# Attention, routed experts and a feed-forward layer on one core: v's two heads of a pair in one product, two v buffers instead of three

## The chip, the cores and the metric

One core of a Trainium2 chip runs the whole program. The metric is device microseconds (us) of one execution, the median of several runs. Five engines work side by side, each through its own list of instructions in order: TensorE (PE, matrix products; its weight loads are shown as PEld), VectorE (DVE), ScalarE (ACT), GpSimd (POOL) and SyncE (SP, which here only starts transfers). They wait for each other through semaphores.

## The reference

```python
# attention: q, k, v of (4 batches, 8 heads, 576 tokens, 64)
q_d, k_d, v_d = mean over groups of 4 tokens        # 144 "downsampled" tokens
out_d  = softmax(scale * q_d @ k_d.T) @ v_d
out_up = repeat(out_d, 4, axis=tokens)
mask   = abs(pos_i - pos_j) < 4
out_local = softmax(where(mask, scale * q @ k.T, -1e9)) @ v
x = (out_up + out_local), heads side by side: (2304, 512)
# routing: each token goes to the expert with the largest cosine logit
y = gate * (relu(x @ w1[e]) @ w2[e])                # 8 experts, 512 -> 1024 -> 512
# feed-forward
h = y @ w_in; out = maximum(0.01 * h, h) @ w_out    # 512 -> 2048 -> 512
```

## The kernel before, in words

The program has two stretches. In the first, the attention and the routing are worked through in 18 tiles of 128 tokens (the four batches laid end to end, 4.5 tiles each). In the second the tokens go expert by expert through the expert layers and then through the feed-forward layer, as long runs of 384- and 512-wide matmuls.

The order of the first stretch is written out by hand in the table ORDER: a list of steps like `LV.6` or `vw.3`, each a call of one function. Each engine runs its share of the steps in the order of the table; transfers of SP too, since they are issued where the step stands. A scheduler does not change it. The steps that matter here:

- `T`, `E`, `P`: q and k are transposed on PE, copied out of PSUM, and added up by fours into qd and kd.
- `ds` is dn_score (L390, L395): downsampled scores of one batch, in two parts; then `dm`, `db`, `dx` (softmax), `dT`, `dv` (dn_pv, L439 and L445: times v_d), `do`, `dh`, `dl` (the result, split into a high part dnh and a low part dnl).
- `S` is lo_score: the local scores. A tile is four strips of 32 queries; each strip meets a window of 38 keys. `SMX` to `SNM` are its softmax, `LT` and `LTE` transpose it into leT, in which the two heads of a pair lie on partitions 0 to 63 and 64 to 127.
- `vw` is load_vw (L319, L323): the windows of v for nine strips (a group, 0 to 7, two per batch) go into one of NVW buffers `vw`, in turn, as 10 or 12 transfers on SP. Head s of a pair lies on partitions 64 s to 64 s + 63. The buffers are set to zero once (L196), since a window fills 48 of 64 partitions. Tile t reads groups 4t // 9 to (4t + 3) // 9: tile 4 reads groups 1 and 2, tile 6 groups 2 and 3, tile 13 groups 5 and 6, tile 15 groups 6 and 7.
- `LV` is lo_pv: the local result of a tile and the repeated downsampled result, added up in one PSUM tile psLV. First the repeat products, with a constant matrix rep_w that copies each downsampled row four times (L554; rows 512 to 575 of a batch, in the four tiles that cross a batch, go through rem_w instead, L559), once for each of the two head halves; then for each of 4 head pairs, 2 heads and 4 strips one small product of leT and vw (L567). A float32 matmul here appears as two records, each a weight load and a pass.
- `LX`, `LAD`: the tile is copied to xt and stored to memory. `SQ`, `X`, `XE`, `L`, `LG`, `LD`, `PF`, `PD`, `SC`: the routing (logits, arg-max, ranks, scattering of the token numbers), for three tiles at a time from `LD` on.
- `WL.u` is w_moe_load for the first expert: SP loads unit u of its weights (two transfers of 512 KB). `WH.u` and `WO.u` split them into a high part (a cast on ACT, L866) and a low part (a subtraction on DVE, L869), in four pieces. The raw weights lie in two buffers, the split ones in four (pools wa and wb, two each).
- `XT`, `XH`, `XO` bring the first tokens of the first expert into place; `L1.f` is its first layer for 128 columns f. `L1.2` and `L1.3` need unit 1.

Of the kernel before, what the change touches and what calls it, by code (L numbers as in the profile page):

```python
# [8 lines left out]
F32 = mybir.dt.float32  # L9
# [44 lines left out]
O = dict(QM=(0, 0, 1, 1), NQ=8, NQD=2, NDE=0, NC=0, NVD=2, NVW=3, NES=3, NW=22, TO=12, TS=11, HB=2, XF=4, XL=3.0, WL=4,  # L54
# [18 lines left out]
E.2.1.1.1 L.3 db.1.1 S.7 SNM.6 LTE.4 LG.3 P.2.1.1 dv.1.0 dx.1.1 ds.2.0 v.2.0 SMX.7 dT.1.1.0 do.1.0 T.2.0.1.1 dE.1.1.0
SSB.7 dT.1.1.1 E.2.0.1.1 dT.1.1.2 dh.1.0 SEX.7 S.8 dm.2.0 dE.1.1.2 dl.1.0 X.1 dE.1.1.1 P.2.0.1 db.2.0 T.3.1.0.0 XE.1
dv.1.1 SMX.8 dx.2.0 E.3.1.0.0 SSB.8 v.2.1 T.3.1.1.0 SSM.7 SEX.8 dT.2.0.0 LAD.1 T.3.1.0.2 do.1.1 LAD.0 dE.2.0.0 ds.2.1
vg.3.0 E.3.1.0.2 E.3.1.1.0 qk.3.0.1 dh.1.1 SSM.8 dT.2.0.1 LAD.2 T.3.1.1.1 dE.2.0.1 dl.1.1 T.3.0.0.0 LAD.3 SNM.8 L.1
vg.3.1 E.3.1.1.1 dm.2.1 T.3.0.0.1 SNM.7 E.3.0.0.0 LV.5 LG.1 E.3.0.0.1 db.2.1 dv.2.0 LX.5 LD.2 v.3.0 dx.2.1 LV.4 LAD.5
# [32 lines left out]
def tile_kernel(ctx, tc, q, k, v, emb, tau, w1, w2, win, wout, out):  # L110
# [51 lines left out]
    with man:  # L162
# [28 lines left out]
        vws = [ac.tile([P, NP, GS, D], F32, name="vw%d" % i) for i in range(O['NVW'])]  # L191
# [119 lines left out]
        def load_vw(g):  # L311
# [3 lines left out]
            for s in range(2):  # L315
                part = t[64 * s:64 * s + 64]
# [67 lines left out]
        def dn_score(b, u):  # L384
            ps = psA.tile([P, 2, 512], F32, name="psD", tag="A")
            idle(ps[:, 0, 0:256], dn_score, b, u)
            for r in range(2):
                for c in range(0, P, 64):
                    for s in range(2):
                        T.matmul(ps[c:c + 64, s, r * GR:(r + 1) * GR], qd[b][64 * s:64 * s + 64, 2 * u + r, c:c + 64],  # L390
                                 kd[b][64 * s:64 * s + 64, 2 * u + r, :], start=True, stop=True)
            if u:
                for n in range(NP):
                    for s in range(2):
                        T.matmul(ps[32 * n:32 * n + 32, s, 2 * GR:3 * GR],  # L395
                                 qd[b][64 * s:64 * s + 64, n, GR - 32:], kd[b][64 * s:64 * s + 64, n, :],
                                 start=True, stop=True)
            sps[b, u] = ps
# [31 lines left out]
        def dn_pv(b, u):  # L430
# [109 lines left out]
        def lo_pv(t):  # L540
# [773 lines left out]
```

## Time and profile before

| | |
|---|---|
| median of 3 runs | 858.31 us (855.56 to 859.88) |
| profiled execution, its own time | 853.95 us |
| its span, first to last instruction | 852.2 us |
| PE busy | 810.4 us (95%), 7887 matmul records |
| DVE, ACT, POOL busy | 462.5, 337.2, 210.7 us |
| mean granted clock of PE | 0.971 |
| DMA | 97.88 MB; 58956 of 104652 packets under 512 B |

The granted clock is 1.0 where PE runs at 2.4 GHz and 0.5 where it runs at 1.2. "Idle before" is the time an engine stood still ahead of an instruction, with what ended it; "issue" means that nothing which the profile shows was awaited.

### The profile page before, as it was taken

How to read it: one execution, taken by the hardware profiler on the slowest of the kernel's cores; microseconds unless marked ns; L12 is line 12 of the kernel's file. 1: busy time of each engine (PE TensorE's matmuls, PEld its weight loads, DVE VectorE, ACT ScalarE, POOL GpSimd, SP SyncE). 2: the span in 40 equal slices, each digit the busy share in tenths (PEclk: the TensorE clock that was granted, in tenths of full speed). 3: DMA queues.
4: the chain of work that ended last, by engine and by line, in shares of the span. 5: the costliest groups of instructions: out<-in, count | busy, mean ns of one | idle time of the engine just before them, and what ended most of it. 6: DMA issues, size and time to landing. Idle time of an engine off the chain costs nothing. (4 is left out here: it accounts for less than half of the span.)

```text
span 852.2 us, 19006 instructions
## 1 busy us (share of the span) xinstructions
PE 810.4 (95%) x7887; PEld 742.1 (87%) x7887; DVE 462.5 (54%) x902; ACT 337.2 (40%) x686; POOL 210.7 (25%) x244
## 2 busy tenths in 40 slices
PE   7878999789999999999999999999999999999995
PEld 6767787679999999999997789999999999999994
DVE  6646655544377988897579992332332232232222
ACT  3445645544454555656433232322223222222221
POOL 8465534234033234323023420101001001001001
PEclk9989978979999999999999999999999999999998
DMA  9779654545476787797634410111011011000001
GB/s 266 172 173 193 157 124 98 140 131 123 102 267 191 258 237 212 237 293 238 211 113 125 136 50 1 37 38 38 1 38 38 0 38 38 1 1 38 0 1 40
DMA packets 104652, 97.88 MB, mean 115 GB/s; under 512 B 58956, under 2 KB 83148, under 8 KB 104562
## 3 DMA queue, kind: packets, MB, share of 16 engines
q1 hardware_dynamic: 94018, 69.88, 29.8%
q0 software_dynamic: 10544, 26.74, 9.9%
q8 instruction: 64, 1.05, 0.5%
q14 instruction: 26, 0.21, 0.1%
HBM read 81.48 MB, written 15.12 MB: 113 GB/s over the span
## 5 line engine op out<-in xcount | busy, mean ns | idle before, releaser
L923 PE MATMUL psh<-xhi,w 128*128 128x384 f32 (+9 forms) x672 | 215.9, 321 | 0.0
L924 PE MATMUL psh<-xlo,w 128*128 128x384 f32 (+9 forms) x672 | 215.6, 321 | 0.0
L925 PE MATMUL psh<-xhi,w 128*128 128x384 f32 (+9 forms) x672 | 215.2, 320 | 0.0
L955 DVE SCALAR_TENSOR_TENSOR hs<-hs 128x384 f32<-128x384 f32 x96 | 61.9, 645 | 185.8 <-ACT hs L954 185.8
L923 PEld LDWEIGHTS psh<-xhi,w 128*128 128x128 f32 x672 | 127.7, 190 | 4.0
L924 PEld LDWEIGHTS psh<-xlo,w 128*128 128x128 f32 x672 | 127.7, 190 | 3.9
L925 PEld LDWEIGHTS psh<-xhi,w 128*128 128x128 f32 x672 | 127.6, 190 | 0.0
L954 ACT COPY hs<-psh 128x384 f32<-128x384 f32 x96 | 45.9, 478 | 194.5 <-PE psh L925 191.6
L1008 PE MATMUL pso<-w,hh 128*128 128x512 f32 x282 | 112.9, 400 | 3.7 <-ACT hh L960 3.1
L1009 PE MATMUL pso<-w,hh 128*128 128x512 f32 x282 | 110.9, 393 | 0.0
L1039 POOL DMA_INDIRECT out_dram<-o,tk x18 | 18.0, 999 | 320.9 <-ACT o L1038 315.4
L869 DVE TENSOR_TENSOR w<-r,w 128x1024 fp32r<-128x1024 f32 (+1 forms) x72 | 83.1, 1159 | 11.0 <-ACT w L866 10.6
L960 ACT CAST hh<-hs 128x384 fp32r<-128x384 f32 x94 | 48.2, 513 | 93.2 <-DVE hs L955 93.2
L996 PE MATMUL psy<-hh,w 128*128 128x192 f32 (+8 forms) x288 | 81.9, 306 | 0.0
L1006 PE MATMUL pso<-w,hl 128*128 128x512 f32 x282 | 80.8, 393 | 0.0
L997 PE MATMUL psy<-hh,w 128*128 128x192 f32 (+8 forms) x288 | 79.4, 298 | 0.0
L911 POOL TENSOR_TENSOR ds<-r 128x512 f32<-128x512 f32 x32 | 42.5, 1327 | 145.8 <-DVE r L909 63.5
L961 DVE TENSOR_TENSOR hl<-hs,hh 128x384 fp32r<-128x384 f32 x94 | 52.4, 557 | 45.8 <-ACT hh L960 45.8
L975 ACT ACTIVATE hh<-psh 128x192 fp32r<-128x192 f32 (+8 forms) x72 | 29.2, 405 | 110.4 <-PE psh L925 107.3
L866 ACT CAST w<-r 128x1024 fp32r<-128x1024 f32 (+1 forms) x72 | 67.6, 947 | 3.5 <-DMA r<-in_moe_w_dram 3.5
L1008 PEld LDWEIGHTS pso<-w,hh 128*128 128x128 f32 x282 | 52.9, 188 | 16.9 <-ACT hh L960 7.9
L1006 PEld LDWEIGHTS pso<-w,hl 128*128 128x128 f32 x282 | 53.0, 188 | 12.9 <-DVE hl L961 0.3
(230 smaller groups left out, 1255.2 us busy)
## 6 DMA issues: line engine op xcount, KB each, us to landing
r<-in_moe_w_dram SPq DMA_DIRECT2D x64, 512.0 KB
r<-in_moe_w_in_dram POOLq DMA_DIRECT2D x16, 512.0 KB, 5.3
r<-in_moe_w_out_dram POOLq DMA_DIRECT2D x16, 512.0 KB, 5.0
vw<-in_v_dram SPq DMA_DIRECT2D x64, 96.0 KB
vg<-in_v_dram SPq DMA_DIRECT2D x8, 576.0 KB
x_d<-xt SPq DMA_DIRECT2D x18, 256.0 KB
yc<-yT_d SPq DMA_DIRECT2D x6, 768.0 KB
qk<-in_q_dram SPq DMA_DIRECT2D x4, 576.0 KB
```

The lines of the kernel that those rows point to most:

```text
L866: A.copy(w[:, 0, i, cs], src)
L869: V.tensor_tensor(out=w[:, 1, i, cs], in0=src, in1=w[:, 0, i, cs].bitcast(F32), op=ALU.subtract)
L923: T.matmul(ps, lh, rh, start=start, stop=False)
L924: T.matmul(ps, lh, rl, start=False, stop=False)
L925: T.matmul(ps, ll, rh, start=False, stop=stop)
L955: V.scalar_tensor_tensor(out=hs, in0=hs, scalar=0.01, in1=hs, op0=ALU.mult, op1=ALU.max)
L961: V.tensor_tensor(out=gl[:, 0:n], in0=hs, in1=gh[:, 0:n].bitcast(F32), op=ALU.subtract)
L996: T.matmul(ps, wh, hh[:, 0:n], start=f == 0, stop=False, skip_group_check=True)
L997: T.matmul(ps, wl, hh[:, 0:n], start=False, stop=False, skip_group_check=True)
L1006: T.matmul(ps, hl[:, c], wh, start=False, stop=f == NF2 - 1, skip_group_check=True)
L1008: T.matmul(ps, hh[:, c], wh, start=f == 0, stop=False, skip_group_check=True)
L1009: T.matmul(ps, hh[:, c], wl, start=False, stop=False, skip_group_check=True)
```

## The change

Four things change together. The buffers of v get a column block for each head of a pair: head 0 fills partitions 0 to 63 of block 0, head 1 partitions 64 to 127 of block 1, and the rest stays zero. One product over all 128 partitions and 128 columns then gives both heads of a pair, where there were two of 64 by 64; the repeat products become 512 (or 128) wide, once instead of once per half, and psLV takes one bank of PSUM instead of two. A buffer is now twice as large, so there are two instead of three (NVW), and the loads of v stand at other places in ORDER. The room for this comes from the split weights of the first stretch: pool wa has one buffer until `cut`, a new pool wc gets the other after it, and the splits of unit 1 (`WH.1`, `WO.1`) stand behind `XH.3`. In dn_score, the products of 64 columns become products of 128.

```diff
-O = dict(..., NVD=2, NVW=3, ...
+O = dict(..., NVD=2, NVW=2, ...
...
-        vws = [ac.tile([P, NP, GS, D], F32, name="vw%d" % i) for i in range(O['NVW'])]
+        vws = [ac.tile([P, NP, GS, 2, D], F32, name="vw%d" % i) for i in range(O['NVW'])]
...
-                part = t[64 * s:64 * s + 64]
+                part = t[64 * s:64 * s + 64, :, :, s]
...
             for r in range(2):
-                for c in range(0, P, 64):
-                    for s in range(2):
-                        T.matmul(ps[c:c + 64, s, r * GR:(r + 1) * GR], qd[b][64 * s:64 * s + 64, 2 * u + r, c:c + 64],
-                                 kd[b][64 * s:64 * s + 64, 2 * u + r, :], start=True, stop=True)
+                for s in range(2):
+                    T.matmul(ps[:, s, r * GR:(r + 1) * GR], qd[b][64 * s:64 * s + 64, 2 * u + r, 0:P],
+                             kd[b][64 * s:64 * s + 64, 2 * u + r, :], start=True, stop=True)
...
-            for s in range(2):
-                for z, (b, r, p0) in enumerate(segs):
-                    for w, src in enumerate((dn_h[b], dn_l[b])):
-                        if r < 4 * P:
-                            T.matmul(ps[:, s, 0:256], rep_w[:, HW + r - p0:HW + r - p0 + P],
-                                     src[:, 0:DM].rearrange("p (i a d) -> p a i d", i=2, a=2)[:, s],
-                                     start=z == 0 and w == 0, stop=False, skip_group_check=True)
-                        else:
-                            for n in range(NP):
-                                T.matmul(ps[:, s, n * D:(n + 1) * D], rem_w[:, n, HW - p0:HW - p0 + P],
-                                         src[:, DM + s * D:DM + (s + 1) * D],
-                                         start=z == 0 and w == 0 and n == 0, stop=False, skip_group_check=True)
+            for z, (b, r, p0) in enumerate(segs):
+                for w, src in enumerate((dn_h[b], dn_l[b])):
+                    first = z == 0 and w == 0
+                    if r < 4 * P:
+                        T.matmul(ps[:, 0], rep_w[:, HW + r - p0:HW + r - p0 + P], src[:, 0:DM],
+                                 start=first, stop=False, skip_group_check=True)
+                    else:
+                        for n in range(NP):
+                            T.matmul(ps[:, 0, 2 * n * D:2 * (n + 1) * D], rem_w[:, n, HW - p0:HW - p0 + P],
+                                     src[:, DM:DM + 2 * D], start=first and n == 0, stop=False, skip_group_check=True)
 
             for n in range(NP):
-                for s in range(2):
-                    for c, b, sg, w0 in strips(t):
-                        w = vwt[b * (NSTRIP // GS) + sg // GS][:, :, sg % GS]
-                        T.matmul(ps[32 * c:32 * c + 32, s, n * D:(n + 1) * D],
-                                 eT[64 * s:64 * s + 64, n, 32 * c:32 * c + 32], w[64 * s:64 * s + 64, n, :],
-                                 start=False, stop=True, skip_group_check=True)
+                for c, b, sg, w0 in strips(t):
+                    w = vwt[b * (NSTRIP // GS) + sg // GS]
+                    T.matmul(ps[32 * c:32 * c + 32, 0, 2 * n * D:2 * (n + 1) * D], eT[:, n, 32 * c:32 * c + 32],
+                             w[:, n, sg % GS].rearrange("p s d -> p (s d)"), start=False, stop=True, skip_group_check=True)
...
-            for nm, bufs in (("wa", 2), ("xa", 1), ("rp", 1)):
+            for nm, bufs in (("wa", 1), ("xa", 1), ("rp", 1)):
...
-            for nm, bufs in (("wb", 2), ("wf", 4), ("rr", 2), ("xb", 1), ("hp", 2)):
+            for nm, bufs in (("wb", 2), ("wf", 4), ("rr", 2), ("xb", 1), ("hp", 2), ("wc", 1)):
...
-                nm = ("wa", "wb")[made["w"] // 2 % 2]
+                nm = ("wa", "wc", "wb", "wb")[made["w"] % 4]
```

The copy to xt and the output of dn_pv follow the new order of the columns. In ORDER, `vw.1` stands where `vw.2` stood, and the later loads stand behind the last tile that reads the buffer they take: `vw.2` behind `LV.2`, `vw.3` behind `LV.4`, `vw.4` behind `LV.6`, `vw.5` behind `LV.7`, `vw.6` behind `LV.11`, `vw.7` behind `LV.13`.

How this moves instructions, at three places. The first is SP's queue around the first expert's weights (r is their raw buffer; vw_111 is buffer 1 of v, regs the register that names the expert; the waits are in brackets). Before, with group 6 of v ahead:

```order
L319 DMA vw_111<-in_v_dram 48x8x64 [waits DMAHW6_49,PE_49]
L323 DMA vw_111<-in_v_dram 48x4x64 [waits DMAHW7_49]
L576 DMA x_d<-xt 128x512 [waits DMAHW0_49,Activation_49]
L576 DMA x_d<-xt 128x512 [waits DMAHW1_49,Activation_49]
L133 TENSOR_LOAD regs [waits DVE_49]
L133 ISA x2
L139 ISA
L139 DMA r_3203<-in_moe_w_dram 128x4x256 [waits DMAHW2_49,Pool_49]
```

Now:

```order
L572 DMA x_d<-xt 128x512 [waits DMAHW4_49,Activation_49]
L572 DMA x_d<-xt 128x512 [waits DMAHW5_49,Activation_49]
L319 DMA vw_111<-in_v_dram 48x8x64 [waits DMAHW6_49,PE_49]
...
L323 DMA vw_111<-in_v_dram 6x4x64 [waits DMAHW1_49]
L133 TENSOR_LOAD regs [waits DVE_49]
L133 ISA x2
L139 ISA
L139 DMA r_2893<-in_moe_w_dram 128x4x256 [waits DMAHW2_49,Pool_49]
```

The twelve transfers of group 7, which wait for PE, now stand between the stores of x and the first expert's weights.

The second is PE's list at tile 6, the products with v (vw_111 and vw_110 are the buffers of groups 2 and 3 before, the other way round now). Before, eight such pairs of lines, of which two:

```order
L567 MATMUL psLV<-vw_111,leT 32x64 x3
L567 MATMUL psLV<-vw_110,leT 32x64 [waits DMAHW1_49]
L567 MATMUL psLV<-vw_111,leT 32x64 x3
L567 MATMUL psLV<-vw_110,leT 32x64 [waits DMAHW7_49]
```

Now there are four:

```order
L563 MATMUL psLV<-vw_110,leT 32x128 x3
L563 MATMUL psLV<-vw_111,leT 32x128 [waits DMAHW7_49,DMAHW1_49]
L563 MATMUL psLV<-vw_110,leT 32x128 x3
L563 MATMUL psLV<-vw_111,leT 32x128 [waits DMAHW2_49,DMAHW0_49]
```

Each of the wide ones waits for the transfers of both heads.

The third is DVE where the first stretch hands over to the first expert (lg, rmx, key, km and oh are the arg-max of the last three tiles; xlo is the low part of the first tokens). Before:

```order
L869 TENSOR_TENSOR w<-r_3203,w 128x512
L818 TENSOR_TENSOR xlo<-psx,xhi 128x192 x3
L624 TENSOR_REDUCE rmx<-lg 128x3
L625 TENSOR_TENSOR lg<-lg,rmx 128x24
L627 SCALAR_TENSOR_TENSOR key<-lg,rev 128x24
L629 TENSOR_REDUCE km<-key 128x3
L631 TENSOR_TENSOR oh<-key,km 128x24
```

Now:

```order
L865 TENSOR_TENSOR w<-r_2893,w 128x512
L814 TENSOR_TENSOR xlo<-psx,xhi 128x192 x3
L865 TENSOR_TENSOR w<-r_2919,w 128x512 x4
L620 TENSOR_REDUCE rmx<-lg 128x3
L621 TENSOR_TENSOR lg<-lg,rmx 128x24
L623 SCALAR_TENSOR_TENSOR key<-lg,rev 128x24
L625 TENSOR_REDUCE km<-key 128x3
L627 TENSOR_TENSOR oh<-key,km 128x24
```

The four subtractions of unit 1 now stand ahead of the arg-max; the four casts on ACT that feed them have moved with them.

## Rows read from the trace of the kernel before

**Rows 1.** Busy time of PE in two stretches: from:to, length, busy (records), clock, DMA.

```profile
0.00:189.00 189.00, 160.56 (x4051) 0.90 0.65 160
189.00:853.00 664.00, 649.85 (x3841) 0.99 0.33 102
```

**Rows 2.** PE's waits up to 189 us: us in total, times, longest.

```profile
PE psLV L567 <- issue: 6.4, 3, 5.1
PE psS L496 <- issue: 4.0, 6, 1.6
PE psL L611 <- issue: 3.4, 1, 3.4
...
PE psDV L439 <- issue: 2.2, 1, 2.2
PE psDV L445 <- issue: 2.0, 2, 1.6
```

**Rows 3.** PE between gaps marked "issue", each stretch from one's end to the next.

```profile
49.30:64.30 15.00, 14.15 (x382) 0.79 0.69 154
...
98.50:108.70 10.20, 8.53 (x255) 1.00 0.39 85
```

**Rows 4.** Timeline of PE, tiles 3 and 16 (start, length); last row, all engines' windows.

```profile
60.63 0.36 PE L554 MATMUL psLV<-dnh,rep_w 128*128 128x256 f32 x1
...
61.28 0.86 PE L567 MATMUL psLV<-vw,leT 64*32 64x64 f32 x64
...
174.02 1.19 PE L567 MATMUL psLV<-vw,leT 64*32 64x64 f32 x64
...
174.00:175.00 1.00, 1.00 (x65) 0.95 (x64) 0.00 (x0) 0.00 (x0) 0.85 (x1) 0.50 0.05 8
```

**Rows 5.** Timeline of PE, products on 128 rows by 64 and 32 columns.

```profile
26.48 2.19 PE L352 MATMUL psT<-ident,qk 128*64 128x128 f32 x36
...
37.32 0.66 PE L445 MATMUL psDV<-vd,deT 128*32 128x65 f32 x32
```

**Rows 6.** Timeline of PE, tiles 4 and 8, which cross a batch.

```profile
90.70 0.63 PE L559 MATMUL psLV<-dnh,rem_w 128*128 128x64 f32 x4
...
93.15 0.30 PE L567 MATMUL psLV<-vw,leT 64*32 64x64 f32 x3
...
110.00 0.39 PE L554 MATMUL psLV<-dnh,rep_w 128*128 128x256 f32 x1
...
114.14 1.19 PE L567 MATMUL psLV<-vw,leT 64*32 64x64 f32 x64
```

**Rows 7.** Timeline of PE, downsampled scores of the second part of batch 0.

```profile
24.02 0.72 PE L390 MATMUL psD<-qkd 64*64 64x144 f32 x16
```

**Rows 8.** Timeline of PE behind tile 4's products, at tile 6's and at tile 13's.

```profile
94.68 0.66 PE L155 MATMUL psX<-ident,xt 128*128 128x128 f32 x4
...
100.41 1.13 PE L567 MATMUL psLV<-vw,leT 64*32 64x64 f32 x64
...
156.83 0.86 PE L567 MATMUL psLV<-vw,leT 64*32 64x64 f32 x64
```

**Rows 9.** Timeline of SP: twelve transfers of a group, then the expert's first weights.

```profile
121.23 1.88 SPq L319 DMA_DIRECT2D vw<-in_v_dram  x4
...
128.67 3.14 SPq L576 DMA_DIRECT2D x_d<-xt  x3
...
156.57 0.41 SPq L139 DMA_DIRECT2D r<-in_moe_w_dram  x1
```

**Rows 10.** Timelines of ACT, PE and DVE at the hand-over to the first expert.

```profile
166.57 0.60 ACT L866 CAST w<-r 128x512 fp32r<-128x512 f32 x1
...
171.90 1.03 PE L611 MATMUL psL<-enT,xT 128*64 128x8 f32 x16 [3.39 <-issue]
...
188.95 0.51 PE L923 MATMUL psh<-xhi,w 128*128 128x192 f32 x1
...
198.58 2.48 DVE L869 TENSOR_TENSOR w<-r,w 128x512 fp32r<-128x512 f32 x4
```

More of the change, by code (lines that the diff above doesn't have):

```diff
@@ L51 @@
 EPS = 1e-9
[L54 removed]
+O = dict(QM=(0, 0, 1, 1), NQ=8, NQD=2, NDE=0, NC=0, NVD=2, NVW=2, NES=3, NW=22, TO=12, TS=11, HB=2, XF=4, XL=3.0, WL=4,
          EC=dict(E00="ACT", E01="DVE", E02="ACT", E10="DVE", E11="ACT", E12="ACT", P0="POOL", P1="DVE", SNM="POOL",
@@ L73 @@
[L73 to L77, printed above, removed]
+E.2.1.1.2 SSB.6 LT.5 XE.2 ds.1.1 RN.2 LTE.5 SEX.6 L.2 dm.1.1 dT.1.0.1 LG.2 T.2.1.1.1 dE.1.0.1 SSM.6 LT.4 E.2.1.1.1 L.3
@@ new lines @@
+db.1.1 S.7 SNM.6 LTE.4 LG.3 P.2.1.1 dv.1.0 dx.1.1 ds.2.0 v.2.0 SMX.7 dT.1.1.0 do.1.0 T.2.0.1.1 dE.1.1.0 SSB.7 dT.1.1.1
+E.2.0.1.1 dT.1.1.2 dh.1.0 SEX.7 S.8 dm.2.0 dE.1.1.2 dl.1.0 X.1 dE.1.1.1 P.2.0.1 db.2.0 T.3.1.0.0 XE.1 dv.1.1 SMX.8
+dx.2.0 E.3.1.0.0 SSB.8 v.2.1 T.3.1.1.0 SSM.7 SEX.8 dT.2.0.0 LAD.1 T.3.1.0.2 do.1.1 LAD.0 dE.2.0.0 ds.2.1 vg.3.0
+E.3.1.0.2 E.3.1.1.0 qk.3.0.1 dh.1.1 SSM.8 dT.2.0.1 LAD.2 T.3.1.1.1 dE.2.0.1 dl.1.1 T.3.0.0.0 LAD.3 SNM.8 L.1 vg.3.1
+E.3.1.1.1 dm.2.1 T.3.0.0.1 SNM.7 E.3.0.0.0 LV.5 LG.1 E.3.0.0.1 db.2.1 dv.2.0 LX.5 LD.2 v.3.0 dx.2.1 LV.4 vw.3 LAD.5
@@ L98 @@
-WO.3.1.0 L2.3 WO.3.0.1 RL.5 RO.5 WO.3.0.0 L1.4 XB L1.7 RL.4 RO.4 L2.4 L1.6 L2.5 GB BT.0 RL.7 RL.6 BT.1 RO.7 BH.0 RO.6
-BT.2 BH.1 BO.0 L2.6 BO.1 BH.2 BO.2 BT.3 L2.7 BH.3 BO.3
+dE.2.1.1 T.3.1.0.1 SMX.11 T.3.1.1.2 E.3.1.0.1 X.6 SSB.11 SNM.9 E.3.1.1.2 dv.2.1 P.3.1.0 v.3.1 SEX.11 P.3.1.1 T.3.0.0.2
+L.5 E.3.0.0.2 LV.8 do.2.1 XE.6 LG.5 LD.5 dh.2.1 L.6 P.3.0.0 LX.8 LT.7 SSM.11 LG.6 T.3.0.1.0 SQ.8 X.8 LM.5 LTE.7 S.10
+dl.2.1 E.3.0.1.0 SNM.11 LAD.8 LV.7 vw.5 LE.5 LAD.6 SMX.10 XE.8 SE.5 SSB.10 L.8 LX.7 ds.3.0 SEX.10 X.7 LG.8 SSM.10 SQ.7
@@ new lines @@
+LT.9 XE.7 SP.8 PF.5 dm.3.0 T.3.0.1.2 LTE.9 S.12 PD.5 SNM.10 E.3.0.1.2 L.7 db.3.0 SC.5 LT.10 LG.7 T.3.0.1.1 SMX.12
+dx.3.0 LV.9 LAD.7 RN.8 early LTE.10 SSB.12 E.3.0.1.1 SEX.12 dT.3.0.0 LD.8 LX.9 LT.11 dE.3.0.0 LV.10 LAD.9 SSM.12
+P.3.0.1 SQ.9 LTE.11 LM.8 S.14 LE.8 LX.10 SE.8 PF.8 SNM.12 X.9 LAD.10 SQ.10 SMX.14 ds.3.1 PD.8 XM XE.9 SSB.14 dT.3.0.1
+SC.8 dm.3.1 LT.12 SEX.14 LV.11 vw.6 dE.3.0.1 SSM.14 LTE.12 db.3.1 X.10 LX.11 dv.3.0 XE.10 SNM.14 X.11 SQ.11 do.3.0 L.9
+dx.3.1 SP.11 S.13 XE.11 RN.11 dT.3.1.0 LG.9 SMX.13 dh.3.0 L.11 dE.3.1.0 SSB.13 dT.3.1.1 LAD.11 dl.3.0 LG.11 dT.3.1.2
@@ new lines @@
+SEX.13 L.10 dE.3.1.1 SSM.13 S.15 dE.3.1.2 SNM.13 LG.10 dv.3.1 LD.11 SMX.15 LT.13 LM.11 SSB.15 LE.11 PF.11 LV.12 do.3.1
+SEX.15 LTE.13 PD.11 dh.3.1 S.16 LX.12 dl.3.1 CF LAD.12 SQ.12 LT.14 SSM.15 LV.13 vw.7 LTE.14 FE SNM.15 X.12 SE.11 LX.13
+WL.0 LT.15 SMX.16 XE.12 SC.11 X.13 WL.1 SSB.16 LTE.15 CS L.12 FC LAD.13 SEX.16 LV.14 SQ.13 SSM.16 LG.12 XE.13 S.17
+LX.14 L.13 SNM.16 LAD.14 SQ.14 SMX.17 X.14 LG.13 SP.14 SSB.17 LT.16 XE.14 LV.15 RN.14 SEX.17 WH.0.0.0 SSM.17 LTE.16
+L.14 WO.0.0.0 SNM.17 WH.0.1.0 LV.16 LX.15 WO.0.1.0 IA WH.0.0.1 X.15 LAD.15 SQ.15 WO.0.0.1 LT.17 LX.16 LAD.16 X.16
@@ new lines @@
+SQ.16 XE.16 XR LTE.17 LG.14 LV.17+15 LD.14 XE.15 PF.14 LM.14 LX.17 L.15 PD.14 L.16 LE.14 LAD.17 cut SQ.17 X.17 SE.14
+LG.15 SP.17 LG.16 XG SC.14 WH.0.1.1 RN.17 XT.0+4 XE.17 XT.1 WO.0.1.1 XH.0 XT.2 WL.2 XH.1 L.17 XO.0 XH.2 XO.1 XT.3 WL.3
+XO.2 LG.17 XH.3 WH.1.0.0 WO.1.0.0 WH.1.0.1 WO.1.0.1 WH.1.1.1 WH.1.1.0 WO.1.1.1 WO.1.1.0 LD.17 XO.3 PF.17+7 LM.17 L1.0
+PD.17 LE.17 SE.17 L1.1 RL.0 SC.17 RO.0 L2.0 RL.1 RO.1 WH.2.0.0 CA L1.2 WO.2.0.0 WH.2.0.1 WH.2.1.0 RK L2.1 WH.2.1.1
+RL.2 L1.3 RO.2 WO.2.0.1 WH.3.0.0 WO.2.1.1 WH.3.1.1 L2.2 WO.2.1.0 WH.3.1.0 RL.3 WO.3.1.1 L1.5 WH.3.0.1 IB RO.3 WO.3.1.0
@@ L100 @@
+L2.3 WO.3.0.1 RL.5 RO.5 WO.3.0.0 L1.4 XB L1.7 RL.4 RO.4 L2.4 L1.6 L2.5 GB BT.0 RL.7 RL.6 BT.1 RO.7 BH.0 RO.6 BT.2 BH.1
+BO.0 L2.6 BO.1 BH.2 BO.2 BT.3 L2.7 BH.3 BO.3
 """
@@ L438, in dn_pv @@
                     for c in range(0, P, 64):
-                        T.matmul(o[c:c + 64, n, :], eT[:, n, kc, c:c + 64], vd[b][:, kc, head(2 * u + n % 2, n // 2), :],
+                        T.matmul(o[c:c + 64, 2 * (n % 2) + n // 2, :], eT[:, n, kc, c:c + 64], vd[b][:, kc, head(2 * u + n % 2, n // 2), :],
                                  start=kc == 0, stop=kc == 1)
@@ L571, in lo_x @@
+            for n in range(NP):
+                for c, b, sg, w0 in strips(t):
+                    w = vwt[b * (NSTRIP // GS) + sg // GS]
+                    T.matmul(ps[32 * c:32 * c + 32, 0, 2 * n * D:2 * (n + 1) * D], eT[:, n, 32 * c:32 * c + 32],
+                             w[:, n, sg % GS].rearrange("p s d -> p (s d)"), start=False, stop=True, skip_group_check=True)
         def lo_x(t):
             x = xt[t] = br.tile([P, DM], F32, name="xt", tag="xt", bufs=4)
-            on("LX").copy(x.rearrange("p (s c) -> p s c", s=2), st_.pop(('V', t))[:, :, 0:256])
+            on("LX").copy(x.rearrange("p (s n d) -> p n s d", s=2, d=D),
+                          st_.pop(('V', t))[:, 0].rearrange("p (n s d) -> p n s d", s=2, d=D))
```

25 lines of the change are left out of this document (3 added, 22 removed).

## The prediction

> **What bounds the kernel now.** First the busy time of TensorE (PE) in the two stretches the work falls into: up to 189 us (attention and routing) it is busy 160.6 of 189 us with 4051 matmul records; after that (experts, feed-forward) 649.9 of 664 us [rows 1]. The change touches the first stretch alone, and what it saves or loses there moves the start of the second, where PE is full, by as much.
>
> Then PE's waits. Of the 28.4 idle us in the first stretch 18.0 stand under "issue" (6.4 + 4.0 + 3.4 + 2.2 + 2.0), 13 times [rows 2]; the ten that are left are waits for data, in small pieces. In "issue" no semaphore is late. From one such gap to the next there are 382 records at one place and 255 at another [rows 3]: three and two times about 127, and so it goes on. A record is a matmul with its weight load, so each stride is some 254 instructions, of the same size each time. I read it as PE waiting for the next block of its own program, in strides that take 5.0 to 5.1 us each where a gap ends them. So PE is the bound in this stretch, partly by its array and partly by how many instructions it has to be handed.
>
> The Trainium skill (Runtime: NRT & Kernel Launch, "Instruction fetch mechanics") says that programs come in blocks of 256 instructions, and that the cost of a boundary is mostly hidden. The trace agrees on the size and not on the cost (18.0 us); by "hidden" the term for program blocks below would be nothing, and the sum 862.0.
>
> **The change part by part.** All times are against the profiled execution (span 852.2, own time 853.95); the median of the three runs is 858.31, 4.4 above it, and I forecast against the median.
>
> *Products with v.* Before, 64 records per tile of 128 tokens, on 64 rows x 32 columns of the array, 64 wide: eight in flight at once. They take 0.86 us at the full clock and 1.19 us where the granted clock is 0.50, which is 1.2 of 2.4 GHz [rows 4]. Now 32 records on 128 rows x 32 columns, 128 wide: four in flight. Half of what they multiply is zeros. Width: 36 records of 128 columns, two in flight, take 2.19 us [rows 5]; less a last drain of some 0.2 that is 55 ns each, 110 ns for one alone. Four abreast: 32 x 110 / 4 = 0.88 us plus some 0.14 for the first to start and the last to drain, 1.02 us; at half clock 0.88 x 2 + 0.14 = 1.9. That four do run abreast on 128 rows is seen in the 32 records of 65 columns that end in 0.66 us [rows 5], 15 to 20 ns each. By the granted clock where each falls, 12 tiles run at the full and 6 at half clock: 12 x 0.16 + 6 x 0.7 = **+6.1 us**. Ends: +2 if no tile falls at half clock, +27 if only two run abreast (32 x 55 ns = 1.8 us, twice that at half clock).
>
> The skill (TensorE: Matmul & The Clock Gate, "The mechanism" in Part 3) has a rule against this change: a weight load overlaps a running matmul only where its row group differs. The new products all cover all rows. The 0.66 us for 32 records on all rows [rows 5] speak against the rule; what it would give is the third rival.
>
> *Repeat products.* 72 records of 256 columns become 36 of 512, and 64 of 64 columns become 32 of 128. A plain tile spends 0.65 us on its four (60.63 to 61.28) [rows 4]; two starts and two drains go: -0.13 for 11 tiles, -0.2 for 3 at half clock, -2.0. The four tiles that cross a batch take 2.45 us at the full clock (90.70 to 93.15) and 4.14 at half (110.00 to 114.14) [rows 6]. Each does the same series twice, once per half of the heads; now once. The 64-column records in it take far longer than 64 columns of the 55 ns per 128 above (16 of them and eight switches fill 2.45 us), so I read them as paced by their weight load and their doubled width as free: almost half of each tile goes, three times -1.0 and once -1.9. Together **-6.9 us**. Ends: -3 if the wider records cost in proportion, -8.
>
> *Downsampled scores.* Eight times 16 records in 0.72 us [rows 7] become 8 on 128 columns, two abreast instead of four: the same array time. **0**; ends -1 and +2 (if the longer weight load shows).
>
> *Program blocks.* The stretch loses 576 + 36 + 32 + 64 = 708 of its 4051 records: 26 strides instead of 32. Work without gaps, 171 us, is now 5.4 us a stride, hardly more than the 5.0 to 5.1 us at which strides come [rows 3]; afterwards 6.5 us. So gaps go by more than their number: I take half, **-9 us**, between -3.2 (in proportion) and -18 (all). Behind the longest gap, 5.1 us [rows 2], the clock is granted at 0.79 over the next 15 us [rows 3]; fewer gaps, fewer such stretches: **-2 us** (ends 0 and -4).
>
> *Two buffers instead of three, loads of v moved.* A load now waits for the last product that reads its buffer; SP waits with it, and what is queued behind it. Group 1 comes earlier, group 2 only after tile 2, long before tile 5 reads it, with batch 3's keys behind it, which also have time. Group 3 waits for tile 4's products, which end at 94.68, and tile 6 needs it at 100.41 [rows 8]. SP takes 7.4 us for such a group (121.23 to 128.67) [rows 9]; the tenth of twelve transfers is needed last, about 5.6 us to issue and an estimated 1.5 to 3 to land (between two and five of its issues, of 0.6 each): 7 to 8.6 us against 5.7, or 4.1 when the 1.6 us gap in between goes [rows 2]. **+2 us** (0 to 4.5). Group 7 waits for tile 13 and is read by tile 15; two tiles' steps, some ten us, lie between, so nothing is lost there. But the first expert's weights now follow it on SP. They were issued at 156.57 [rows 9], a microsecond before tile 13's products end (156.83 + 0.86) [rows 8]; now 7.4 us after those, at about 165. ScalarE (ACT), whose first split of them stood at 166.57 [rows 10], will wait 3 to 5 us there, and behind it leT of tile 16 and xt of tile 15. Before, PE stood 3.4 us in a gap at this very place, to 171.90 [rows 10], which covers it; without that gap part of the wait shows: **+2 us** (0 to 5).
>
> *Splits of unit 1 behind the hand-over.* Four casts on ACT and four subtractions on VectorE (DVE) move ahead of the last tile group's arg-max, on which the ranks and, behind them on PE, the first expert's first matmul wait, now at 188.95 [rows 10]. One cast of 0.60 and four subtractions of 2.48 us [rows 10] make 3.1 us in front of it; at their old place two casts stood ahead of tile 17's leT, which comes some 0.6 us earlier. **+2.5 us** (0 to 3.5). That the weights of unit 3 are then issued 3 us later costs nothing: their splits stand behind two more steps of the first expert.
>
> *The rest.* Memset of vw: two of 4608 elements for three of 2304 is 2 us more on DVE, ahead of two copies; I take 0, as PE's waits for data in this stretch are elsewhere small (ends 0 and +2). The copy to xt has as many elements: 0. Bytes of v are the same.
>
> **Sum:** 6.1 - 6.9 + 0 - 9 - 2 + 2 + 2 + 2.5 = -5.3. On the profiled 853.95 that is 848.7; on the median, **853.0 us**. The case's own range is 847 to 856.
>
> **The rivals.**
> 1. *Gains and prices cancel.* Gaps go only in proportion (-3.2) because where a gap ends, another wait stood behind it: in the 5.1 us of the longest one the loads and DVE also caught up. Clock 0, the rest as above: +2.5, 860.8; where it holds in part, 857 to 860. For it: the gaps are uneven, two of them, 5.1 and 3.4, make 8.5 of the 18.0 us. Against it: waits for data are small in this stretch [rows 2].
> 2. *Slower: the queue on SP decides.* The loads held back by two buffers, and the expert weights behind the last of them, become PE's new wait: +4.5 at tile 6, +5 on ACT, +3.5 at the hand-over, and idle PE falls to the half clock, where the products cost most. With -5 for program blocks: 6.1 - 6.9 - 5 + 4.5 + 5 + 3.5 = +7.2, 865.5. It decides when the tenth transfer of group 3 lands over 10 us after tile 4, or the first weights land after 171. Against it: the ten us that group 7 has, and the gap that covers ACT.
> 3. *The products do not overlap.* If a load on all rows waits for the product in flight, they run one by one: 32 x 110 = 3.5 us per tile at the full clock and 7 at half, 12 x 2.7 + 6 x 5.8 = +67, in place of the +6.1 of the sum: 914. (This is what the skill's rule on row groups would bring.) The rows for 128 rows x 32 columns (0.66 us for 32) speak plainly against it [rows 5].
> 4. *All gaps go*, with the half clock behind them: -18 - 4 instead of -9 - 2: 842.
>
> **Chances.** A difference under 0.5% (4.3 us) cannot be told from none. Forecast 0.42 (nine tenths of it counts as faster, or 0.38, since its upper edge reaches 856), cancel 0.33, slower by SP's queue 0.17, no overlap 0.03, all gaps 0.05. So faster 0.38 + 0.06 (all gaps, and an edge of cancel) = 0.44, slower 0.03 + 0.17 + 0.01 = 0.21, same 0.35. The range goes from 845, below the forecast's own low edge, to 866, so that it takes in rival 2 as priced; rivals 3 and 4 and what lies beyond rival 2's price, together some 0.17, are left out.
>
> **What will show it.** Steps right: v's products near 1.0 us at the full clock and 1.9 at half; batch-crossing tiles near 1.4 us for their repeats; "issue" before PE some 9 us in the first stretch, with strides of the same 127 records; a DMA wait of about 2 us at tile 6; the first expert's first matmul near 184. Wrong: products over 1.5 us at the full clock (no fourfold overlap); "issue" still above 15 us (gaps do not follow from the count); a wait for vw or for the expert weights above 5 us; the first expert's start not moved though PE has less to do.

## The result and the profile after

The changed kernel takes 847.16 us (median of 6 runs, 843.62 to 852.25), the kernel before 859.1 beside it: a ratio of 0.988 (95% interval 0.983 to 0.992), 7 to 14 us less. Forecast were 853.0, with 845 to 866 as the range: right in sign and range, at its fast edge in size. Beside before once more, in another set of runs, the ratio was 0.990 (below). Runs over 1.5% above the fastest of the same kernel are left out of all medians and ratios here (four of twelve of the copies in set 3, one of twelve of both order moves in set 2, one of before in each set).

PE's busy time of the profile after, up to the first expert's first matmul and from there on (from:to, length, busy (records) of PE, PEld, DVE, ACT, POOL, then clock, DMA share, GB/s):

```profile
0.00:182.40 182.40, 155.56 (x3343) 125.82 (x3343) 109.85 (x283) 94.97 (x218) 94.38 (x136) 0.92 0.68 167
182.40:844.60 662.20, 648.81 (x3841) 603.78 (x3839) 355.18 (x619) 241.94 (x468) 116.61 (x108) 0.99 0.33 102
```

The first expert starts 6.55 us earlier than in [rows 10]; the second part is 1 us shorter (662.2 us against 663.25, from 188.95 to the end of the span). So of the 7.6 us between these two profiled executions nearly all was won in front. The other 4.3 us between the medians are in no profile: before's profiled execution (853.95) lies 5 us under its median, after's (846.37) 1 us under its own. PE is busy 5.0 us less with 708 records fewer. What it waited for there (total, times, longest):

```profile
PE psLV L563 <- DMA vw<-in_v_dram: 7.5, 4, 5.6
PE psR L651 <- DVE oh L627: 2.6, 1, 2.6
PE psX L155 <- issue: 2.5, 1, 2.5
PE psLV L563 <- issue: 2.1, 2, 1.6
PE psS L495 <- issue: 1.9, 1, 1.9
...
PE psR L180 <- ACT lg L610: 1.5, 1, 1.5
```

Against [rows 2], "issue" went from 18.0 to 7.4 us. New are 7.5 us for v's strips and 4.1 in front of the hand-over (arg-max 2.6, logits 1.5). So PE won 5.0 of busy time and 10.6 of gaps, and gave 9.0 back in waits for data: 6.6. On PE's timeline (start, length, line, tile, shapes, count, [idle before]), with tile 3, the batch-crossing tile 4, tile 6, tile 16 and the hand-over:

```profile
55.45 0.48 PE L553 MATMUL psLV<-dnh,rep_w 128*128 128x512 f32 x1
55.77 0.40 PE L553 MATMUL psLV<-dnl,rep_w 128*128 128x512 f32 x1
56.10 1.08 PE L563 MATMUL psLV<-vw,leT 128*32 128x128 f32 x32
...
82.23 0.66 PE L557 MATMUL psLV<-dnh,rem_w 128*128 128x128 f32 x4
82.73 0.61 PE L557 MATMUL psLV<-dnl,rem_w 128*128 128x128 f32 x4
83.18 0.45 PE L553 MATMUL psLV<-dnh,rep_w 128*128 128x512 f32 x1
83.46 0.40 PE L553 MATMUL psLV<-dnl,rep_w 128*128 128x512 f32 x1
83.79 1.08 PE L563 MATMUL psLV<-vw,leT 128*32 128x128 f32 x32
...
88.80 0.42 PE L563 MATMUL psLV<-vw,leT 128*32 128x128 f32 x6
94.85 1.08 PE L563 MATMUL psLV<-vw,leT 128*32 128x128 f32 x16 [5.63 <-DMA vw<-in_v_dram]
...
162.95 1.94 PE L563 MATMUL psLV<-vw,leT 128*32 128x128 f32 x32
...
182.28 0.18 PE L651 MATMUL psR<-oh,tri 128*128 128x24 bf16 x1 [2.57 <-DVE oh L627]
```

A plain tile's repeats take 0.65 us (55.45 to 56.10), what they took before [rows 4]. A crossing tile's take 1.56 (82.23 to 83.79) instead of 2.45 [rows 6]. The products with v take 1.08 us and 1.94 at half clock, for 0.86 and 1.19 [rows 4]; the next work starts some 0.07 before the last of them ends. Four of them do run abreast: 32 in 1.08 us, where one by one, at the 110 ns that the prediction gives one alone, they would take 3.5.

### The profile page after: what moved, and what is told of

Its sections match the earlier page's. It is cut to its first block, busy times and chain, and to the rows that moved or that the text cites. A ratio compares the mean times of both kernels' runs of the same rounds, so it can differ in the third digit from the quotient of the medians.

```text
span 844.6 us, 17621 instructions
## 1 busy us (share of the span) xinstructions
PE 804.4 (95%) x7179; PEld 729.6 (86%) x7179; DVE 465.0 (55%) x901; ACT 336.9 (40%) x686; POOL 211.0 (25%) x244
```

## Experiments

Three sets of runs, each on one chip with the kernel before beside it; before took 857.0, 846.2 and 854.0 us there, so medians are compared within a set and ratios to before only with care between sets. The table gives each profile up to the first expert's first matmul; "issue" and "v" add up the rows of PE's waits with that releaser, and "tile 4 at" is the start of tile 4's repeats.

Each row is one execution, and one differs from the next. Eight of them (after, tile 6 later, arg-max first, and after, both order moves and copies added in their two sets) have the same program up to tile 4's repeats and reach them between 82.0 and 88.1 us, with 1.9 to 6.8 us of issue before them. An edit that acts later has no part in that, so what it does is read from tile 4 on. From there to the first expert after's two profiles take 100.2 and 91.7 us.

| kernel (set) | time, us | ratio to before (95%) | tile 4 at | first expert at | records | PE busy | issue | v |
|---|---|---|---|---|---|---|---|---|
| before | 859.1 | 1 | 90.7 | 188.95 | 4050 | 160.5 | 18.0 | 0 |
| after | 847.2 | 0.988 (0.983 to 0.992) | 82.2 | 182.4 | 3343 | 155.6 | 7.4 | 7.5 |
| moves alone (1) | 856.7 | 1.000 (0.997 to 1.003) | 86.2 | 197.0 | 4051 | 164.6 | 11.0 | 5.4 |
| tiny products added (1) | 858.8 | 1.003 (1.000 to 1.006) | 86.0 | 195.0 | 3918 | 164.4 | 14.3 | 5.0 |
| tile 6 later (1) | 846.7 | 0.990 (0.984 to 0.995) | 88.1 | 183.3 | 3342 | 157.0 | 14.3 | 1.1 |
| arg-max first (1) | 844.8 | 0.986 (0.981 to 0.992) | 85.6 | 177.85 | 3342 | 155.1 | 11.2 | 1.7 |
| old repeats (2) | 843.5 | 0.997 (0.995 to 1.000) | 82.3 | 176.8 | 3411 | 155.7 | 5.7 | 4.3 |
| copies added (2) | 855.8 | 1.011 (1.007 to 1.014) | 86.0 | 186.1 | 3343 | 160.3 | 10.1 | 3.8 |
| both order moves (2) | 839.3 | 0.991 (0.987 to 0.994) | 82.0 | 170.4 | 3342 | 152.3 | 4.8 | 3.7 |
| more merged (2) | 844.1 | 0.997 (0.995 to 1.000) | 88.4 | 180.2 | 3070 | 166.1 | 3.6 | 3.7 |
| after (3) | 845.7 | 0.990 (0.987 to 0.994) | 84.5 | 176.2 | 3343 | 153.6 | 6.4 | 1.0 |
| both order moves (3) | 840.8 | 0.984 (0.980 to 0.989) | 82.2 | 171.0 | 3343 | 154.4 | 7.7 | 0 |
| moves alone (3) | 853.9 | 1.001 (0.998 to 1.004) | 87.7 | 191.6 | 4051 | 165.1 | 12.9 | 3.0 |
| copies added (3) | 853.6 | 0.999 (0.995 to 1.003) | 83.7 | 181.6 | 3342 | 156.4 | 11.1 | 0.9 |

**The moves alone.** The kernel before, with the new order, two buffers of v in their old layout, and the new places of the weights:

```diff
-O = dict(... NVW=3, ...)
+O = dict(... NVW=2, ...)     (and the order of the change)
-for nm, bufs in (("wa", 2), ("xa", 1), ("rp", 1)):
+for nm, bufs in (("wa", 1), ("xa", 1), ("rp", 1)):     ("wc", 1 opened at the cut)
```

> The kernel before with only the moves of the change: its order of the work, two buffers of v and the place of unit 1's weights; products, repeat products and downsampled scores stay those of before. Theory A (the gain is PE's own work and the delivery of its program: fewer records, fewer gaps): nothing of the gain is here, only the prices. Gaps marked issue stay at 15 to 21 us in the first stretch (before 18.0, after 7.4), a DMA wait for v at tile 6 of 2 to 7 us, some 3 to 4 us in front of the hand-over; about 866 us (862 to 871). Theory B (the moved loads and splits bring the gain): faster than before, 846 to 853.

Measured: no change, and again none in set 3, where after ran beside it:

> The kernel before with the order, the two buffers and the weight places of the change, but its own products, again, beside after. As in the first set: within 0.5% of before; after lies 8 to 12 us under it, all of it from the merged products.

> The kernel after, unchanged, beside the next three on one chip, since the time of before differs between chips (857 and 846 us in the two sets so far). If the gain is PE's own work (some 5 us less busy up to the first expert) and gaps come on top: 0.984 to 0.993 of before on this chip too, nearer 0.99 where before has fewer gaps.

After lies 8.2 us under the moves alone. So, to within 0.3% of the time, none of the gain comes from the moved loads and splits (theory B falls): with them in place, it comes from the merged products. What is merged (products with v, repeat products, downsampled scores, and with them psLV's one bank of PSUM for two) was not told apart by time. The price that theory A put on the moves (866 us) doesn't come either, nor do its 15 to 21 us of gaps: there are 11.0 and 12.9. PE's waits in the moves alone, set 3:

```profile
PE psS L496 <- issue: 5.4, 2, 4.7
PE psLV L567 <- issue: 3.4, 9, 0.5
PE psLV L567 <- DMA vw<-in_v_dram: 3.0, 3, 1.3
PE psR L655 <- DVE oh L631: 2.9, 1, 2.9
PE psL L611 <- issue: 2.8, 4, 1.7
```

With before's records, gaps and waits for v come to 16.4 and 15.9 us where before had 18.0 and 0: as if the one took the other's place. (PE also ran at a lower mean clock, 0.86 and 0.87 against 0.90, beside some 4 us more of busy time.)

**Tiny products added.** To after's products with v, 32 more per tile of tokens, 8 columns wide:

```diff
+for n in range(NP):
+    for c in range(0, P, 32):
+        T.matmul(ps[c:c + 32, 1, 0:8], ones[:, 0:32], dum[:, 0:8], start=True, stop=True)
+        T.matmul(ps[c:c + 32, 1, 0:8], ones[:, 0:32], dum[:, 0:8], start=True, stop=True)
```

> The kernel after, with 32 tiny products per tile of tokens (8 columns wide, into the half of psLV that is now unused), 576 records in all and no other work. They add array time of their own: by 11 to 25 ns a record (the 64 records of 38 columns in 0.77 us; the rank products 25 to 35 ns apart) 6 to 14 us. Theory A (gaps follow the count of records): the gaps marked issue go from 7.4 us back to 13 to 18, first matmul of the first expert at 193 to 204 instead of 182.4, 858 to 868 us. Rival (gaps do not follow the count; they went because other waits changed): issue stays under 9 us, first expert at 188 to 196, only the array time is added.

576 records add 8.8 us of busy time and bring issue from 7.4 to 14.3; the first expert starts at 195.0. That lies in theory A's ranges, but 195.0 lies in the rival's too, and issue alone is one profile of each: kernels with after's 3343 records show 4.8 to 14.3 without any added traffic. So the count doesn't set the gaps by itself, and what part it has in them this run doesn't show.

**Copies added.** After, with four copies of 1 MB in HBM that nothing reads; PE's program is unchanged:

```diff
+def traffic(i):
+    for j in (2 * i, 2 * i + 1):
+        nc.sync.dma_start(out=scratch[256 * j:256 * j + 256], in_=w1[j, 0:256, :])
-... vw.4 ... vw.5 ...
+... vw.4 dd.0 ... vw.5 dd.1 ...
```

> The kernel after, with four copies of 1 MB each from HBM to HBM added, two behind the loads of group 4 of v and two behind those of group 5 (issued near 121 and 139 us), whose result nothing reads. PE's program is the same to the instruction. Theory A (a gap is a program block that queues behind data on the DMA engines): gaps marked issue between 115 and 160 us go up by 3 to 10 us (after: 0.38 + 0.34 + 0.44 + 0.19 + 2.54 + 1.63), each behind a block transfer that starts late; 850 to 857 us. Rival (gaps are set by PE's own pace and count alone): issue there stays within 1 us of after's; what is lost stands as waits for v or other data.

> The kernel after with the four copies of 1 MB, again, beside after. If gaps are program blocks that queue behind data: 4 to 12 us over after, issue of PE up to the first expert 2 us or more above that of after's run here. If not: within 3 us of after.

Beside after (set 3) it takes 7.9 us more. The first forecast of the gaps failed: in set 2 issue between 115 and 160 us was 3.5 us, where after has 5.5, and not 3 to 10 us more. (Of the 5.5, 2.5 are the gap at psX, which is no program block, as said below.) The copies went out at 101 and 117 us (103 and 116 in set 2), earlier than that expectation said. In set 3 the gaps from 100 to 160 us are 6.9 us in all, in after's run of the same set 1.2. The two large ones on PE's timeline:

```profile
104.95 0.75 PE L501 MATMUL psS<-qkT 64*32 64x38 f32 x62
108.18 0.23 PE L501 MATMUL psS<-qkT 64*32 64x38 f32 x2 [2.48 <-issue]
...
125.67 1.07 PE L569 MATMUL psLV<-vw,leT 128*32 128x128 f32 x30
130.02 0.41 PE L569 MATMUL psLV<-vw,leT 128*32 128x128 f32 x2 [3.27 <-issue]
```

PE stops after 62 of 64 scores and after 30 of 32 products, inside a series that waits for nothing new. In set 2 it stopped at the second place too, for 3.47 us; the gaps of after's two profiles near that place are 0.44 and 0.30 us:

```profile
130.12 0.64 PE L569 MATMUL psLV<-vw,leT 128*32 128x128 f32 x2 [3.47 <-issue]
```

```profile
130.40 0.28 PE L563 MATMUL psLV<-vw,leT 128*32 128x128 f32 x1 [0.44 <-issue]
```

```profile
124.64 0.41 PE L563 MATMUL psLV<-vw,leT 128*32 128x128 f32 x3 [0.30 <-issue]
```

And each large gap of set 3 holds exactly one transfer of the instruction queue (packets, MB, share of 16 engines; here the gap that ends at 130.02):

```profile
q1 hardware_dynamic: 419, 0.75, 60.7%
q8 instruction: 1, 0.02, 1.7%
```

In the kernel before it was the same: one such transfer, and data packets for 95.9% of the engines' time, inside its longest gap [rows 2]. Between 600 and 700 us before's PE fetched four of them and was busy 100.00 of 100 us, with the DMA engines at 0.08. So "issue" at these places is a program block that comes late because data is ahead of it on the DMA engines; the copies show it at the second place, in both sets, and the packets in the gaps agree with it. Not every gap is one: in the traces 16.6 of before's 18.0 us end 1.2 to 1.6 us after such a transfer has landed, and 3.5 of after's 7.4.

The Trainium skill (Runtime: NRT & Kernel Launch, "Instruction fetch mechanics") calls the cost of a block's boundary mostly hidden. The trace agrees for 600 to 700 us and not for the stretch with the busy DMA engines.

**The wait for v, and the arg-max.** Two edits of after's order, each alone and then together:

```diff
-... PD.2 LV.6 ... vw.4 LX.6 ... SQ.6 ... X.6 ... P.3.1.1 T.3.0.0.2 L.5 ...
+... PD.2 ... vw.4 ... P.3.1.1 LV.6 T.3.0.0.2 LX.6 SQ.6 X.6 L.5 ...
-... XH.3 WH.1.0.0 ... WO.1.1.0 LD.17 XO.3 ...
+... XH.3 LD.17 WH.1.0.0 ... WO.1.1.0 XO.3 ...
```

> The kernel after, with tile 6's products with v (and what follows from them on ACT and PE: xt, squares, transposes) moved in the order of the work behind the last q and k of batch 3 that stood after them, just ahead of tile 8's. Theory A (the wait of 6.9 us for group 3 of v is a plain loss that other work can cover): DMA wait for v under 1.5 us, the half clock behind it gone, first expert at 173 to 178 instead of 182.4, 838 to 843 us. Rival (the wait is where the program's blocks catch up, or where tile 6's logits are due): the waits come back as issue or as waits for logits, 845 to 849 us.

> The kernel after, with the arg-max of the last tile group ahead of the splits of unit 1's weights (one step moved on DVE). Theory A (the splits in front of it cost 2.5 to 3 us at the hand-over): PE's wait for the arg-max goes from 2.6 to under 0.5 us, first expert's first matmul 2 to 3 us earlier against what precedes it, 843 to 845 us. Rival (the first expert then waits as long for unit 1's splits): a wait for w in front of the first expert's second unit, 847 us.

In "tile 6 later" alone, group 4 is loaded ahead of tile 6's products, over strips that they still read, so tile 6 is computed from other rows of v; the amount of work is the same. Its wait for v goes from 7.5 to 1.1 us, issue from 7.4 to 14.3, and the first expert starts no earlier (183.3). Its time lies in the rival's range, and its ratio is no better than after's. But that the wait came back as issue isn't shown: 6.8 of the 14.3 us lie before tile 4, ahead of the edit, where after has 1.9. Behind it issue is 7.4 us, against 5.5 and 2.4 in after's two profiles.

With the arg-max moved its wait is gone from the list. Up to the hand-over that kernel's program is after's, so most of the 4.5 us by which its first expert starts earlier (it also waits 5.8 us less for v and 3.8 us more on issue) is the difference of one execution from another; the arg-max's own part is the 2.6 us. By time alone (0.986 against 0.988 and 0.990) no gain can be told.

> The kernel after with both moves of order: the arg-max of the last tile group ahead of unit 1's splits, and tile 6's products with v just ahead of tile 8's (group 4 of v then loaded behind them). Theory A (the wait for group 3 of v is a loss by itself): first expert at 171 to 176 us, 836 to 841 us. Theory C (where PE doesn't wait for v there, the next program block is late instead, since both queue on the same DMA engines at that time): v's wait gone but issue up by about as much; not better than the arg-max moved alone, 843 to 847.

> The kernel after with the arg-max moved and tile 6's products moved, again, beside after. If the two moves are worth what the first set and the traces say: 5 to 9 us under after on the same chip. If only the arg-max counts: 2 to 3 us under it.

Together (group 4 now loaded behind tile 6): 840.8 beside after's 845.7 in set 3, 4.9 us less, with intervals that just overlap. It is the fastest kernel of the study by its median. The 839.3 us of set 2 lie in theory A's range, but before ran 11 us faster there than in set 1, from which the range was worked out. Between theories A and C the runs don't decide: in set 3 after waits only 1.0 us for v, so that there was little to remove, and in set 2 3.7 us of the wait are left. Nor did issue rise: 2.6 of its 7.7 us in set 3 stand at psX, where after's profile puts 2.5 us down to ACT, so without this place it is 5.1 against 6.4. Of its 5.2 us at the first expert, 2.3 stand at tile 4 already, ahead of both moves; the other 2.9 are about the 3.2 of the arg-max at the hand-over. On PE's timeline now:

```profile
169.39 1.65 PE L180 MATMUL psR<-dum,ones 128*128 128x256 bf16 x7 [1.32 <-ACT lg L610]
170.84 0.22 PE L651 MATMUL psR<-oh,tri 128*128 128x24 bf16 x1
```

The 2.57 us in front of L651 in after (3.19 in its profile of set 3) are gone.

**The repeat products alone put back.** After, with each series twice for half of the columns:

```diff
-T.matmul(ps[:, 0], ..., src[:, 0:DM], ...)
+for h in range(2):
+    T.matmul(ps[:, 0, 256 * h:256 * h + 256], ..., src[:, 256 * h:256 * h + 256], ...)
```

(and the remainder's products 64 wide, once per head.)

> The kernel after with the repeat products of before (each series twice, for half of the columns; 256 and 64 wide), all else as after: 68 records more. Theory A (the doubled width is nearly free where the weight load paces): the four tiles that cross a batch take 2.4 us for their repeats instead of 1.5, plain ones 0.65 as in either kernel; PE busy up by 3.5 to 5 us, 850 to 854 us. Rival (the term of 6.9 in the prediction holds): busy up by 6 to 8 us, 854 to 857.

Its crossing tile on PE's timeline:

```profile
82.25 0.63 PE L558 MATMUL psLV<-dnh,rem_w 128*128 128x64 f32 x4
...
83.48 0.53 PE L558 MATMUL psLV<-dnh,rem_w 128*128 128x64 f32 x4
...
84.70 0.54 PE L565 MATMUL psLV<-vw,leT 128*32 128x128 f32 x12
```

2.45 us (82.25 to 84.70) against after's 1.56: 0.9 for each of four tiles at full clock. A plain tile takes 0.63 to 0.67 in either kernel. Theory A's reading holds tile by tile. In the sums it doesn't show as clearly. PE's busy time is 3.4 us above that of "both order moves" in its set (152.3), which fits the 3.6, but only 0.2 and 2.1 us above after's two profiles, whose mean clock was lower (0.92 and 0.94 against 0.96). The time, 843.5 us, lies under both forecasts, in a set where before was faster too; after itself didn't run in that set, so the whole time can't be set against it.

**More merged.** After with the arg-max moved, and logits and downsampled products with v each made one product on 128 columns instead of two on 64:

```diff
-for c in range(0, P, 64):
-    T.matmul(ps[c:c + 64, 0:E], xT[t][:, kk, c:c + 64], enT[:, kk, :], ...)
+T.matmul(ps[:, 0:E], xT[t][:, kk], enT[:, kk, :], ...)
```

> The kernel after with the arg-max moved, and two more pairs of products made one as the change did with the downsampled scores: logits (64 to 128 wide in their tokens, 288 to 144 records) and the downsampled products with v (256 to 128). 272 records fewer, two blocks of program. Theory A (fewer records, fewer late blocks): issue under 9 us (11.2 with the arg-max moved alone), 838 to 843 us. Rival (array time grows as concurrency goes, and gaps are a matter of when data moves, not of count): issue 9 to 13, 844 to 847 us.

Each theory held in half: with 272 records fewer issue is down to 3.6 us, as A said, and the time lies in the rival's range. The kernel is 4.8 us slower than "both order moves" in its set, which differs from it in the place of tile 6's products too. Groups of PE up to the first expert, "both order moves" first, then "more merged" (count | busy, mean ns):

```profile
L607 PE MATMUL psL<-enT,xT 128*64 128x8 f32 x288 | 12.1, 211 | 0.2 <-ACT xT L600 0.2
```

```profile
L605 PE MATMUL psL<-enT,xT 128*128 128x8 f32 x144 | 20.7, 271 | 0.4 <-ACT xT L599 0.4
```

Half the records cost 8.6 us more here, and 6.1 more in the other pair (7.5 and 6.3 against "arg-max first", whose order it has). Two products on 64 columns run abreast, one on 128 runs alone. On PE's timeline a tile's logits went from 40 to 120 ns a record:

```profile
97.98 0.64 PE L607 MATMUL psL<-enT,xT 128*64 128x8 f32 x16
```

```profile
108.00 0.96 PE L605 MATMUL psL<-enT,xT 128*128 128x8 f32 x8
```

The Trainium skill (TensorE: Matmul & The Clock Gate, "The mechanism" in Part 3) says a weight load overlaps a running matmul only where its row group differs. Products on all rows and all columns fit that here (120 ns for 8 columns); the change's products, on all rows and a quarter of the columns, don't (32 of 128 columns in 1.08 us).

## Why the prediction was right, and where it was not

- *Products with v* (+6.1): 18.0 us became 23.7, +5.7 (21.8, +3.8, in after's second profile). The lengths were right (1.02 forecast for 1.08 to the end of the last, 1.9 for 1.94), and they overlap on all rows, so rival 3 falls. That the sum agrees is in part luck: six tiles were forecast at the half clock, and only tiles 6 and 15, in part, and 16 ran at it; a tile at full clock costs 0.22 us more and not 0.16, and tiles 6 and 15, cut in pieces by waits, took 2.8 and 2.4 us.
- *Repeat products* (-6.9): the crossing tiles gave 0.9 each at full clock and 2.6 at tile 8, which fell at the half clock before and no longer does: 5.3. Plain tiles gave nothing, not 0.13 to 0.2: two wide products take as long as four narrow ones, so that part of the term was wrong.
- *Downsampled scores* (0): eight records in 0.76 us for sixteen in 0.72 [rows 7].
- *Program blocks and clock* (-9 and -2): gaps -10.6, or -11.6 in after's second profile; the mean clock of the stretch 0.92 and 0.94 against 0.90. The size of the gaps was right, the mechanism not. The clock gave back more than 2 us, it seems: the two terms above come to +0.4 us, PE's busy time fell by 5.0, and among products that the change left alone those at psX went from 14.0 to 12.5 us and those at psLT from 14.0 to 12.1. "Strides that take 5.0 to 5.1 us each" was read as a fixed pace of delivery; the copies show that a block is late when data is on the DMA engines. That the fewer records took the gaps away isn't shown either: with all of before's records the moves alone already have 11.0 and 12.9 us of them for 18.0. Nor are all 7.4 us late blocks: the 2.5 us at psX follow ACT's copy of tile 13's xt, which ended as PE went on.
- *Two buffers* (+2, up to 4.5): the step that failed most. It cost 7.5 us in one profile and 1.0 in the next of the same kernel, and 1.7 in "arg-max first", which is the same program there. The group's time on SP was taken from [rows 9], where little else moved. Here it went out at 84 us, among batch 3's loads, on SP's timeline:

```profile
84.38 1.94 SPq L319 DMA_DIRECT2D vw<-in_v_dram  x4
86.41 0.94 SPq L323 DMA_DIRECT2D vw<-in_v_dram  x2
87.40 5.86 SPq L319 DMA_DIRECT2D vw<-in_v_dram  x4
93.30 0.86 SPq L323 DMA_DIRECT2D vw<-in_v_dram  x2
```

  9.8 us for the twelve instead of 7.4, and tile 6's last products ran at 97.81, 12.9 us after tile 4's ended at 84.87; forecast were 7 to 8.6.
- *First expert's weights behind group 7* (+2): ACT waited 4.3 us for them (forecast 3 to 5), 1.4 in after's second profile. Little of it reached PE: for leT, which stands behind it on ACT, PE waited 0 and 0.3 us.
- *Splits of unit 1* (+2.5): 2.6 us of wait for the arg-max, 3.2 in the second profile; moving it took them away. Confirmed.

The prices of data waits summed to 9.0 instead of 6.5, gaps and busy time to -15.6 instead of -11.8: -6.6 to the first expert where -5.3 was forecast. The medians gave -12 and, in set 3, -8.3; of the -12 the profiles show 7.6. Rival 1 (gaps and prices cancel) described the moves alone, not the change. Rival 2 found its place right (SP's loads of v are late) and its price in one profile of two; it doesn't decide: after is faster than before with 7.5 us of that wait and with 1.0.

## What to carry to other kernels

Merge two products into one where the halves ran one after the other: the crossing tiles' repeats gave 0.9 us each. Leave them apart where they ran abreast on halves of the columns: a smaller count of records didn't pay for the lost overlap. In between lie products on a quarter of the columns, as those with v: merged they took 0.22 us a tile more at full clock, and what their fewer records gave back was not measured alone.

Before pricing a gap marked "issue", look for a stop in the middle of a series and for the instruction queue's transfer inside it. Such gaps grew with busier DMA engines and an unchanged program of PE, so moving data away from that time is worth trying, though no run here shows that it cures them. Don't add up two waits that hang on the same DMA engines before you have tested the removal of one: what comes of it was not settled here.

Before you read an edit's worth from two profiles, look where they part. The same program differed by 6 us at tile 4, before the edit had acted, and that is more than most of the edits were worth.

## What was not expected of the hardware

- Program blocks share the DMA engines with the data closely enough that 4 MB of copies cost the kernel 7.9 us, with 5.7 us more of PE's gaps between 100 and 160 us than in after's profile of the same set.
- The same kernel before took 846.2 to 859.1 us by set, more than the change brings. Sets 2 and 3 have the same chip number on record and still differ by 7.8 us, so only runs of one set tell 1% apart; what differs between sets stays open.
- ACT stood 4.7 to 4.8 us before it copied tile 13's xt in five profiles (after twice, both order moves and copies added in set 3, tile 6 later), with a releaser that the profile doesn't name and, in after's, with PE's products done 2.9 us earlier by their modelled ends. The trace's semaphore changes have the wait end with one of PE's, at 149.49 in after. That points to PE itself being late there, with the 2.5 us at psX behind it; why stays open.
